# Attention and a gated feed-forward block on one core: first batch's q loaded whole behind k, its kv products and norms in another order

## The chip, the cores and the metric

The kernel runs on one core of a Trainium2 chip. The metric is the device time of one execution in microseconds (us). The core has a matrix engine (TensorE, PE in the profile, whose weight loads are listed apart as PEld), VectorE (DVE), ScalarE (ACT), GpSimd (POOL) and SyncE (SP), which here only issues transfers. TensorE writes to PSUM, a small memory from which DVE and ACT read; everything else lies in SBUF. Transfers from and to main memory run on 16 DMA engines, which the queues of SP, ACT and POOL share.

## The reference

```
kv  = einsum('bhsd,bhse->bhde', k, v)          # 8 batches, 8 heads, 576 rows, 64 wide
out = einsum('bhsd,bhde->bhse', q, kv)
rms = sqrt(mean(out*out, -1) + 1e-6)
x   = (out / rms * g_norm) as (4608, 512)
xn  = x / sqrt(mean(x*x, -1) + 1e-6) * moe_rms_g
h   = silu(xn @ w_gate) * (xn @ w_val)         # 512 -> 1536
y   = h @ w_out                                # 1536 -> 512
```

Inputs and output are float32; the kernel's matrix products take bfloat16.

## The kernel before, in words

Each batch's 576 rows are taken as four chunks of 128 rows (512 rows, "main") and a rest of 64. The 8 heads go in four pairs j = 0 to 3; P0 is pairs 0 and 1 (heads H0, 0 to 3), P1 is pairs 2 and 3 (H1, 4 to 7). The feed-forward block works on groups of 512 rows, one group for each batch and a ninth for the rests. Its weights come in four blocks of three 128-column slices (`wg`, `wv`, each loaded and cast to bfloat16 by transfers of the POOL queue), wo likewise.

In the steady part a list of slots, each a gate or value product or a part of the output product, is run in order on TensorE, and a planner (`Placer`) puts the pieces of the next batch's attention into slots by cost. The change does not touch that part. It touches the lead, lines 814 to 931, where the order is written out by hand (`manual_schedule`): an engine runs its instructions in the order in which the code issues them.

Batch 0's lead, in the order of the code: POOL issues the loads of v's rest (`vr`, "remv") and v's main part in two halves of heads, cast on the way (814, 815). SP loads k's heads H0, ACT k's H1 (816, 817), then SP q's chunks 0 and 1 of all heads (818), ACT the rest of k (`krst`) and the gains (`grow`). The second half of q's columns (chunks 2 and 3) follows on SP and ACT (826 to 828) with a dependency: not before v's rest has landed. POOL then makes the identities, issues the eight weight loads (832) and clears some tiles (833 to 836).

TensorE turns over an idle tile (`spin`, 844 and inside `kv_pairs`) until v is there. Then: kv of P0 in one PSUM tile (`kva`, 850), q's chunks 0 and 1 turned for both halves (`qa`, `qb`, 851), the gains turned (`gT`), kv of P1 in one tile (`kvb`, 854). DVE masks kv to its diagonal blocks on the way out (`kv_pairs_out`, kvs). `oT_mm` makes the transposed attention output, which ACT squares (`sqT_`); `stat_pairs` sums the squares by head into a PSUM tile `st`, over a guard product that holds the epsilon; `lead_chain` turns these sums into one factor `al` per row and head (reciprocal, product, sum, product on DVE, square root on ACT, reciprocal on DVE); `o_pairs` makes the output again in row order, `xna_pairs` scales it, `xT_mm` turns it, and `xT_out` writes x with the gain. All of this is for chunks 0 and 1 only. The gates of the first three slices on these 256 rows (`gates`, line 712) follow at once.

Chunks 2 and 3 come behind: `early` is a list of 22 half-width gate and value slots in the order gates of block 0, values of block 0, gates of block 1 and so on, and `behind(n)` issues a piece of their attention behind slot n: at 0 the late q is turned (`qT_mm(ALL, (2, 3))`) and copied, at 2 and 3 oT and its squares, at 5 the sums, at 5 to 9 the chain of scales (`steps`), at 7 and 8 o, at 11 and 12 xna, at 14 and 15 xT. POOL casts the late q (887, 888) and issues batch 1's loads (889 to 891) ahead of wo's.

PSUM pools: `mm1` three tiles, `o2` two, `att` three; a tile is taken again when its last reader is done.

Of the kernel before, what the change touches and what calls it, by code (L numbers as in the profile page):

```python
# [10 lines left out]
FP32 = mybir.dt.float32  # L11
# [3 lines left out]
OP = mybir.AluOpType  # L15
ACT = mybir.ActivationFunctionType
SYNC = mybir.DependencyInfo(mybir.DependencyClass.Sync, mybir.DependencyReason.DATA)
# [70 lines left out]
def kernel(  # L88
# [12 lines left out]
    nc = tc.nc  # L101
    B, H, S, D = q.shape
    d_model = H * D
    d_ff = moe_w_gate.shape[1]
    eps = 1e-6
    NC = 4
    MAIN = 128 * NC
    REM = S - MAIN
    NS = d_model // 128
# [8 lines left out]
    pool = lambda name, bufs, **kw: ctx.enter_context(tc.tile_pool(name=name, bufs=bufs, **kw))  # L118
# [13 lines left out]
    mm1_p = pool("mm1", 3, space=bass.MemoryType.PSUM)  # L132
    o2_p = pool("o2", 2, space=bass.MemoryType.PSUM)
    att_p = pool("att", 3, space=bass.MemoryType.PSUM)
# [8 lines left out]
    gall = consts.tile([128, NS + 1], FP32, name="gall")  # L143
    vc, kc = ([consts.tile([128, H, (NC + 1) * D], BF16, name=f"{t}c{n}") for n in range(2)] for t in "vk")
    sel = consts.tile([128, 2, 2], BF16, name="sel")
    qc = consts.tile([128, H, (NC + 1) * D], BF16, name="qc1")
    diag = consts.tile([128, 2 * D], BF16, name="diag")
    ones = consts.tile([1, 128], FP32, name="ones")
    epsr = consts.tile([1, (NC + 1) * H], FP32, name="epsr")
    gain = consts.tile([128, NS], FP32, name="gain")  # L150
# [5 lines left out]
    kvs = [consts.tile([128, NS, 2, D], BF16, name=f"kvs{n}") for n in range(3)]  # L156
# [24 lines left out]
    def load_main(b, t, heads=(0, H), cs=(0, NC), queue=nc.sync):  # L181
        if (b, t) not in staged:
            staged[b, t] = stage.tile([128, H, NC * D], FP32, name="stg")
        h0, h1 = heads
        view = src[t][b, :, 0:MAIN, :].rearrange("h (p c) d -> p h (c d)", c=NC)
        return queue.dma_start(
            out=staged[b, t][:, h0:h1, cs[0] * D : cs[1] * D], in_=view[:, h0:h1, cs[0] * D : cs[1] * D]
        )
# [17 lines left out]
    def cast_main(b, t, eng, heads=(0, H), cs=(0, NC)):  # L206
        if (b, t) not in mains:
            mains[b, t] = qkv.tile([128, NC, H, D], BF16, name=f"main_{'qkv'[t]}")
        h0, h1 = heads
        copy = eng.copy if eng is nc.scalar else eng.tensor_copy  # L210
        return copy(  # L211
            out=mains[b, t][:, cs[0] : cs[1], h0:h1, :],
            in_=staged[b, t].rearrange("p h (c d) -> p c h d", c=NC)[:, cs[0] : cs[1], h0:h1, :],
        )
# [23 lines left out]
    def spin(ps, n):  # L238
        for _ in range(n):
            nc.tensor.matmul(ps, lhsT=idle[:, :128], rhs=idle[:, : ps.shape[-1]], start=True, stop=True, skip_group_check=True)  # L240
# [4 lines left out]
    class Att:  # L245
# [34 lines left out]
                            start=c == 0, stop=c == NC, skip_group_check=True,  # L280
                        )

        def kv_pairs(self, js, wait=0):
            ps = mm1_p.tile([128, 4, 2 * D], FP32, name="mm1")
            spin(flat(ps), wait)
            ps = ps[:, : len(js)]
            for i, j in enumerate(js):
                for c in range(NC + 2):
                    h = slice(2 * j, 2 * j + 2)
                    if c < NC:  # L290
                        k_, v_ = self.pair(1, c, j), self.pair(2, c, j)
                    else:
                        k_, v_ = krT[:, c - NC, h, :], vr[:, h, c - NC, :]
                    nc.tensor.matmul(
                        ps[:, i, :], lhsT=k_, rhs=v_,
                        start=i == 0 and c == 0, stop=i == len(js) - 1 and c == NC + 1, skip_group_check=True,
                    )
            return ps
# [121 lines left out]
            src = ps.rearrange("p j (c t) -> p j c t", t=128)  # L420
            nc.scalar.activation(out=to, in_=src, func=ACT.Square)

        def stat_pairs(self, js, c0, c1, pool, name, guard=False):
            first = self.st is None
            if first:
                self.st = pool.tile([128, 2, NC + 1, H], FP32, name=name)
                if guard:
                    nc.tensor.matmul(
                        self.st[:, 0, c0:c1, :], lhsT=ones, rhs=epsr[:, : (c1 - c0) * H], start=True, stop=True,
                        skip_group_check=True,  # L430
                    )
                    first = False
            for c in range(c0, c1):
                for j in js:
                    nc.tensor.matmul(
                        self.st[:, :, c, 2 * j : 2 * j + 2], lhsT=self.sqT[:, j, c], rhs=sel,
                        start=first, stop=True, skip_group_check=True,
                    )
                    first = False
# [370 lines left out]
    V, G, A = nc.vector, nc.gpsimd, nc.scalar  # L810
# [2 lines left out]
    ALL = range(NS)  # L813
    v_loads = [G.dma_start(out=vr[: REM // 2].rearrange("p h c d -> p h (c d)"), in_=two(2))]
    v_loads += [load_cast(0, 2, hsx) for hsx in (H0, H1)]
    load_main(0, 1, H0)
    load_main(0, 1, H1, queue=A)
    load_main(0, 0, cs=(0, 2))
    krst = stage.tile([128, H, NC * D], FP32, name="stg")[: REM // 2, :, : 2 * D]
    A.dma_start(out=krst, in_=two(1))  # L820
    A.preload_act_table(ACT.Sqrt)
# [1 line left out]
    for half in range(2):  # L823
        A.dma_start(out=grow[NS : NS + 1, half * D : (half + 1) * D], in_=g_norm.rearrange("(o d) -> o d", o=1))

    for hsx, queue in ((H0, nc.sync), (H1, A)):
        rest = load_main(0, 0, hsx, cs=(2, 4), queue=queue)
        tc.add_manual_dep(rest.ins, v_loads[0].ins.name, SYNC, reason="k and v have the queues first")

    make_identity(nc, ident)  # L830
    make_identity(nc, identf)
    w_loads = [load_w(n) for n in range(len(FB))]
    G.memset(kvs[0], 0.0)
    G.memset(kvs[1], 0.0)
    for tile_ in (kc[0], kc[1], vc[0], vc[1], qc):
        G.memset(tile_[REM:, :, NC * D :], 0.0)

    def fold(w, s, eng):
        if eng == "ACT":
# [1 line left out]
        else:  # L841
            V.tensor_scalar(out=w[:, s], in0=w[:, s], scalar1=gain[:, s : s + 1], scalar2=None, op0=OP.mult)

    spin(mm1_p.tile([128, MAIN], FP32, name="mm1"), 18)
    a = Att(0)
    cast_main(0, 1, V, H0)
    cast_main(0, 1, A, H1)
    V.tensor_copy(out=krT[: REM // 2], in_=krst.rearrange("p h (c d) -> p c h d", c=2))
    cast_main(0, 0, V, cs=(0, 2))
    kva = a.kv_pairs(P0, 4)  # L850
    qa, qb = (a.qT_mm(js, (0, 1)) for js in (P0, P1))
    gT = o2_p.tile([128, NS + 1], FP32, name="o2")
    nc.tensor.matmul(gT, lhsT=grow, rhs=identf, is_transpose=True, start=True, stop=True, skip_group_check=True)
    kvb = a.kv_pairs(P1)
    for i, j in enumerate(P0):
        a.kv_pairs_out(kva, i, j)
    a.qT_out(qa, P0, 0, A)
    a.qT_out(qb, P1, 0, V)
    V.tensor_copy(out=gall, in_=gT)
    gcol = gall[:, NS : NS + 1]  # L860
    for half in range(2):
        rows = slice(half * D, (half + 1) * D)
        V.tensor_tensor(out=sel[rows, 1, half : half + 1], in0=gcol[rows], in1=gcol[rows], op=OP.mult)
    ta = a.oT_mm(P0, 0, 2, o2_p)
    a.sqT_(ta, P0, 0, 2)
    for i, j in enumerate(P1):
        a.kv_pairs_out(kvb, i, j)
    V.tensor_scalar(
        out=gain, in0=gall[:, 0:NS], scalar1=gcol, scalar2=float(d_model) ** 0.5, op0=OP.mult, op1=OP.mult
    )  # L870
    for i, j in enumerate(P1):
        a.sqT_(a.oT_mm((j,), 0, 2, (o2_p, mm1_p)[i], 4 * (1 - i)), (j,), 0, 2)
    a.stat_pairs(P0, 0, 2, mm1_p, "mm1", guard=True)
    a.stat_pairs(P1, 0, 2, mm1_p, "mm1")
    ox = a.o_pairs(P0, 0, 2, att_p, "att")
    oy = a.o_pairs(P1, 0, 2, att_p, "att")
    a.lead_chain(0, 2)
    spin(mm1_p.tile([128, MAIN], FP32, name="mm1"), 5)
    for o, js in ((ox, P0), (oy, P1)):
        for i, j in enumerate(js):  # L880
            a.xna_pairs(o[:, :, 2 * i : 2 * i + 2], (j,), 0, 2)

    for j, pool_, eng in zip(ALL, (o2_p, o2_p, None, None), (A, V, A, V)):
        a.xT_mm((j,), (0, 1), pool_)
        a.xT_out(j, (0, 1), eng)

    for hsx in (H0, H1):
        cast_main(0, 0, G, hsx, cs=(2, 4))
    for t in (0, 2, 1):
        load_cast(1, t, (0, H))  # L890
        load_cast(1, t)
# [10 lines left out]
        early += [slots_a(0, j, 0, half)[0] for j in js if n] + [slots_a(0, j, 0, half)[1] for j in js]  # L902
    held = {}

    steps = {5: (0, 4), 7: (4, 6), 8: (6, 8), 9: (8, 12)}

    def behind(n):
        if n == 0:
            ps = a.qT_mm(ALL, (2, 3))
            a.qT_out(ps[:, 0:2], P0, 2, V)  # L910
            a.qT_out(ps[:, 2:4], P1, 2, V)
        elif n in (2, 3):
            js = (P0, P1)[n - 2]
            a.sqT_(a.oT_mm(js, 2, 4, o2_p), js, 2, 4)
        elif n == 5:
            a.st = None
            a.stat_pairs(P0, 2, 4, att_p, "att")
            a.stat_pairs(P1, 2, 4, att_p, "att")
        if n in steps:
            for f in a.chain(2, NC)[slice(*steps[n])]:  # L920
                f()
        if n in (7, 8):
            held[n - 7] = a.o_pairs((P0, P1)[n - 7], 2, 4, att_p, "att")
        if n in (11, 12):
            i = (11, 12).index(n)
            a.xna_pairs(held[i], (P0, P1)[i], 2, 4)
        elif n in (14, 15):
            i = (14, 15).index(n)
            a.xT_mm((P0, P1)[i], (2, 3), None if i else o2_p)
            for j in (P0, P1)[i]:  # L930
                a.xT_out(j, (2, 3), A)
# [83 lines left out]
```

## Time and profile before

| | |
|---|---|
| median of 3 runs | 322.69 us (321.81 to 322.73) |
| the profiled execution | 321.78 us |
| its span in the profile | 320.0 us |
| TensorE busy | 313.0 us (98%) |
| VectorE, ScalarE, GpSimd busy | 176.3, 142.3, 90.8 us |
| granted TensorE clock | 1.00 |
| DMA moved | 40.57 MB, mean 127 GB/s |

The span is what the profile covers; 1.78 us of the execution lie around it. A busy share is an average over the whole span: the lead is some 5% of it and has limits of its own, so what the change is worth is read from the first 30 us. In a timeline line the columns are start, length, engine, source line, operation, out<-in with tile names, shape and count, and in brackets the engine's idle time before it and what ended that. Lines such as L684 are helpers' lines: the product of gates and values stands there whoever calls it.

### The profile page before, as it was taken

To read this page: it belongs to the slowest core of one execution; us is meant where nothing else is said; L and a number is where in the kernel's file an instruction comes from. 1 tells how busy PE (TensorE), PEld (TensorE's weight loads), DVE (VectorE), ACT (ScalarE), POOL (GpSimd) and SP (SyncE) were. 2 spreads that over 40 slices of the span, in tenths; PEclk is the share of its full clock that TensorE was granted. 3 is DMA by queue.
4 is the path that set the end of the run, shared out by engine and by line. 5 is a ranking of instruction groups with operands and counts; after the bars stand their busy time and mean duration, and the time that the engine had idled before them with its cause. 6 is when DMAs were issued, how large, how long until landed. Compare 5 with 4: busy or idle time off the path is not lost.

```text
span 320.0 us, 5586 instructions
## 1 busy us (share of the span) xinstructions
PE 313.0 (98%) x2142; PEld 159.3 (50%) x2142; DVE 176.3 (55%) x395; ACT 142.3 (44%) x263; POOL 90.8 (28%) x113
## 2 busy tenths in 40 slices
PE   8799999999999999999999999999999999999996
PEld 3588865444454445444444444444444444444443
DVE  4665538589949661967186817691778043203410
ACT  1465456486668323832292228322742233223321
POOL 8753530069008500860077006800510000000000
PEclk9999999999999999999999999999999999999999
DMA  8999999999783985497549955995000600040002
GB/s 215 221 203 197 195 230 209 200 214 110 141 206 93 155 165 144 113 146 147 137 149 123 155 146 154 105 139 151 34 3 0 172 35 0 6 106 21 0 33 100
DMA packets 78934, 40.57 MB, mean 127 GB/s; under 512 B 42552, under 2 KB 74428, under 8 KB 78908
## 3 DMA queue, kind: packets, MB, share of 16 engines
q0 software_dynamic: 31200, 14.22, 34.9%
q1 hardware_dynamic: 46224, 25.01, 32.0%
q10 hardware_dynamic: 1484, 0.99, 1.0%
q8 instruction: 17, 0.28, 0.4%
q14 instruction: 9, 0.07, 0.1%
HBM read 37.78 MB, written 9.44 MB: 148 GB/s over the span
## 4 chain that ended last, share of the span: by engine, by line
PE 91%; DMA 8%; issue 0%; DVE 0%; ACT 0%; POOLq 0%
PE mm L684 57%; PE o L719 27%; DMA wv<-in_moe_w_val_dram 5%; DMA remv<-in_v_dram 2%; PE att L278 2%; PE mm L719 2%; PE att L349 1%; PE o L362 1%; PE att L362 0%; PE mm L746 0%; PE o L746 0%; PE att L324 0%; PE att L558 0%; PE att L410 0%; PE att L445 0%
## 5 line engine op out<-in xcount | busy, mean ns | idle before, releaser
L702 DVE TENSOR_TENSOR h<-silu,mm 128x512 bf16<-128x512 bf16 (+1 forms) x120 | 75.4, 630 | 84.6 <-PE mm L684 75.2
L693 ACT ACTIVATE silu<-mm 128x512 bf16<-128x512 f32 (+1 forms) x120 | 66.5, 557 | 83.2 <-PE mm L684 74.3
L684 PE MATMUL mm<-x,wv 128*128 128x512 bf16 (+1 forms) x432 | 99.9, 356 | 0.2 <-DMA wv<-in_moe_w_val_dram 0.2
L684 PE MATMUL mm<-x,wg 128*128 128x512 bf16 (+1 forms) x420 | 97.9, 358 | 0.0
L719 PE MATMUL o<-wo,h 128*128 128x512 bf16 x396 | 90.0, 379 | 0.0
L452 POOL TENSOR_TENSOR sq<-sq,g 128x512 bf16<-128x512 bf16 x31 | 35.4, 1151 | 126.5 <-ACT sq L397 126.5
L684 PEld LDWEIGHTS <-wv 128*128 128x128 bf16 x480 | 46.2, 98 | 45.4 <-DMA wv<-in_moe_w_val_dram 0.5
L684 PEld LDWEIGHTS <-wg 128*128 128x128 bf16 x468 | 45.1, 98 | 44.9 <-DMA wg<-in_moe_w_gate_dram 0.2
L719 PEld LDWEIGHTS <-h 128*128 128x128 bf16 x420 | 40.2, 98 | 45.8
L735 ACT COPY osb<-o 128x512 f32<-128x512 f32 x33 | 19.2, 586 | 69.2 <-PE o L719 67.2
L460 DVE TENSOR_REDUCE st<-sq 128x8 f32<-128x512 bf16 x62 | 39.7, 677 | 0.2
L307 DVE CAST kvs<-att 64x256 bf16<-64x256 f32 x14 | 5.9, 422 | 28.7 <-PE att L278 28.1
L527 DVE TENSOR_TENSOR xna<-outa,al 128x512 bf16<-128x512 bf16 x24 | 15.1, 683 | 0.0
L684 PE MATMUL mm<-xr,wv 128*128 128x512 bf16 x48 | 12.3, 379 | 0.0
L684 PE MATMUL mm<-xr,wg 128*128 128x512 bf16 x48 | 12.3, 379 | 0.0
L397 ACT ACTIVATE sq<-att 128x512 bf16<-128x512 f32 x19 | 11.7, 618 | 0.0
L401 ACT CAST outa<-att 128x512 bf16<-128x512 f32 x19 | 11.5, 604 | 0.0
L211 POOL CAST main_q<-stg 128x1024 bf16<-128x1024 f32 (+1 forms) x12 | 11.3, 971 | 0.6 <-DMA stg<-in_q_dram 0.6
L240 PE MATMUL mm<-idle 128*128 128x512 bf16 x27 | 8.7, 492 | 1.2 <-DVE idle L138 1.2
L840 ACT ACTIVATE wv<-wv,gain 128x384 bf16<-128x384 bf16 x16 | 9.0, 608 | 0.4 <-PE mm L684 0.4
L197 POOL DMA_DIRECT2D vc<-in_v_dram x9 | 7.7, 860 | 0.3 <-DMA wg<-in_moe_w_gate_dram 0.3
L719 PE MATMUL mm<-wo,h 128*128 128x512 bf16 x24 | 7.8, 379 | 0.0
(138 smaller groups left out, 187.6 us busy)
## 6 DMA issues: line engine op xcount, KB each, us to landing
out_dram<-osb SPq DMA_DIRECT2D x31, 256.0 KB, 2.5
stg<-in_q_dram SPq DMA_DIRECT2D x6, 1024.0 KB, 7.9
vc<-in_v_dram POOLq DMA_DIRECT2D x7, 512.0 KB, 8.1
kc<-in_k_dram POOLq DMA_DIRECT2D x7, 512.0 KB, 6.4
wg<-in_moe_w_gate_dram POOLq DMA_DIRECT2D x4, 384.0 KB, 14.9
wv<-in_moe_w_val_dram POOLq DMA_DIRECT2D x4, 384.0 KB, 16.2
wo<-in_moe_w_out_dram POOLq DMA_DIRECT2D x4, 384.0 KB, 13.0
out_dram<-osb SPq DMA_DIRECT2D x9, 128.0 KB, 2.3
```

Source lines behind the costliest of these rows:

```text
L211: return copy(out=mains[b, t][:, cs[0] : cs[1], h0:h1, :], in_=staged[b, t].rearrange("p h (c d) -> p c h d", c=NC)[:, cs[0] : cs[1], h0:h ...
L397: nc.scalar.activation(out=self.sq[c][:, 0], in_=self.o_of(c), func=ACT.Square)
L401: nc.scalar.copy(out=self.outa[c], in_=self.o_of(c))
L452: eng.tensor_tensor(out=self.sq[c][:, 1], in0=self.sq[c][:, 0], in1=g2, op=OP.mult)
L460: nc.vector.reduce_sum(out=self.part(self.st[:, which], c), in_=of, axis=AX.X)
L527: return eng.tensor_tensor(out=self.part(self.xna, c), in0=self.outa[c].rearrange("p (c h) d -> p c h d", c=2), in1=self.part(self.al, c). ...
L684: nc.tensor.matmul(ps[:, : c1 - c0], lhsT=w[n][:, s, jj * 128 : (jj + 1) * 128], rhs=x_of(g, s, c0, c1), start=s == 0, stop=s == NS - 1)
L693: nc.scalar.activation(out=sis[g, j][:, c0:c1], in_=ps, func=ACT.Silu)
L702: nc.vector.tensor_tensor(out=hs[g, j][:, c0:c1], in0=sis[g, j][:, c0:c1], in1=v_ps, op=OP.mult)
L719: nc.tensor.matmul(ps, lhsT=hs[g, j][:, t * 128 : (t + 1) * 128], rhs=wo[j // OB][:, j % OB, :], start=j == 0, stop=j == NF - 1)
L735: (eng.copy if eng is nc.scalar else eng.tensor_copy)(out=o, in_=ps)
L840: A.mul(out=w[:, s], in_=w[:, s], mul=gain[:, s : s + 1])
```

## The change

q of batch 0 is loaded whole, in two halves of heads on SP, right behind k, which is loaded in four quarters of two heads that alternate between SP and ACT; the dependency on v's rest is gone. The casts of q's chunks 0 and 1 are split by heads between DVE and ACT; chunks 2 and 3 are cast by POOL right after the weight issues, the gain is computed on POOL instead of DVE, and the clearing of tiles moves behind the lead. TensorE's order becomes: kv of P0, q of P0 turned, gT, the guard, q of P1 turned, oT of P0, kv of pair 2 and of pair 3 in a tile each (one from `mm1`, one from `att`), oT of each, the sums, o, then the late q turned, then spins (3 instead of 5; 24 instead of 18 at the start, and the 4 ahead of pair 2's oT are gone). xT is made by pairs of heads in `o2` tiles. The copies of the late q stand behind xT's. The pieces behind the early slots move up by one to two slots.

```diff
-        def kv_pairs(self, js, wait=0):
-            ps = mm1_p.tile([128, 4, 2 * D], FP32, name="mm1")
+        def kv_pairs(self, js, wait=0, pool=None):
+            ps = (pool or mm1_p).tile([128, 4, 2 * D], FP32, name="att" if pool else "mm1")
...
-        def stat_pairs(self, js, c0, c1, pool, name, guard=False):
+        def guard(self, c0, c1):
+            self.st = mm1_p.tile([128, 2, NC + 1, H], FP32, name="mm1")
+            nc.tensor.matmul(
+                self.st[:, 0, c0:c1, :], lhsT=ones, rhs=epsr[:, : (c1 - c0) * H], start=True, stop=True,
+                skip_group_check=True,
+            )
+
+        def stat_pairs(self, js, c0, c1):
             first = self.st is None
             if first:
-                self.st = pool.tile([128, 2, NC + 1, H], FP32, name=name)
-                if guard:
-                    nc.tensor.matmul(
-                        self.st[:, 0, c0:c1, :], lhsT=ones, rhs=epsr[:, : (c1 - c0) * H], start=True, stop=True,
-                        skip_group_check=True,
-                    )
-                    first = False
+                self.st = att_p.tile([128, 2, NC + 1, H], FP32, name="att")
...
-    load_main(0, 1, H0)
-    load_main(0, 1, H1, queue=A)
-    load_main(0, 0, cs=(0, 2))
+    for n in range(NS):
+        load_main(0, 1, (2 * n, 2 * n + 2), queue=A if n % 2 else nc.sync)
+    for hsx in (H0, H1):
+        load_main(0, 0, hsx)
...
-    for hsx, queue in ((H0, nc.sync), (H1, A)):
-        rest = load_main(0, 0, hsx, cs=(2, 4), queue=queue)
-        tc.add_manual_dep(rest.ins, v_loads[0].ins.name, SYNC, reason="k and v have the queues first")
-
     make_identity(nc, ident)
     make_identity(nc, identf)
     w_loads = [load_w(n) for n in range(len(FB))]
-    G.memset(kvs[0], 0.0)
-    G.memset(kvs[1], 0.0)
-    for tile_ in (kc[0], kc[1], vc[0], vc[1], qc):
-        G.memset(tile_[REM:, :, NC * D :], 0.0)
...
-    spin(mm1_p.tile([128, MAIN], FP32, name="mm1"), 18)
+    spin(mm1_p.tile([128, MAIN], FP32, name="mm1"), 24)
...
-    cast_main(0, 0, V, cs=(0, 2))
+    cast_main(0, 0, V, H0, cs=(0, 2))
+    cast_main(0, 0, A, H1, cs=(0, 2))
     kva = a.kv_pairs(P0, 4)
-    qa, qb = (a.qT_mm(js, (0, 1)) for js in (P0, P1))
+    qa = a.qT_mm(P0, (0, 1))
     gT = o2_p.tile([128, NS + 1], FP32, name="o2")
     nc.tensor.matmul(gT, lhsT=grow, rhs=identf, is_transpose=True, start=True, stop=True, skip_group_check=True)
-    kvb = a.kv_pairs(P1)
+    a.guard(0, 2)
+    qb = a.qT_mm(P1, (0, 1))
     for i, j in enumerate(P0):
         a.kv_pairs_out(kva, i, j)
-    a.qT_out(qa, P0, 0, A)
-    a.qT_out(qb, P1, 0, V)
+    a.qT_out(qa, P0, 0, V)
     V.tensor_copy(out=gall, in_=gT)
     gcol = gall[:, NS : NS + 1]
+    G.tensor_scalar(
+        out=gain, in0=gall[:, 0:NS], scalar1=gcol, scalar2=float(d_model) ** 0.5, op0=OP.mult, op1=OP.mult
+    )
+    for hsx in (H0, H1):
+        cast_main(0, 0, G, hsx, cs=(2, 4))
+    a.qT_out(qb, P1, 0, V)
+    a.sqT_(a.oT_mm(P0, 0, 2, o2_p), P0, 0, 2)
+    made = [a.kv_pairs((j,), pool=pool_) for j, pool_ in zip(P1, (None, att_p))]
+    for ps, j in zip(made, P1):
+        a.kv_pairs_out(ps, 0, j)
...
-    ta = a.oT_mm(P0, 0, 2, o2_p)
-    a.sqT_(ta, P0, 0, 2)
-    for i, j in enumerate(P1):
-        a.kv_pairs_out(kvb, i, j)
-    V.tensor_scalar(
-        out=gain, in0=gall[:, 0:NS], scalar1=gcol, scalar2=float(d_model) ** 0.5, op0=OP.mult, op1=OP.mult
-    )
-    for i, j in enumerate(P1):
-        a.sqT_(a.oT_mm((j,), 0, 2, (o2_p, mm1_p)[i], 4 * (1 - i)), (j,), 0, 2)
-    a.stat_pairs(P0, 0, 2, mm1_p, "mm1", guard=True)
-    a.stat_pairs(P1, 0, 2, mm1_p, "mm1")
+    for j, pool_ in zip(P1, (o2_p, mm1_p)):
+        a.sqT_(a.oT_mm((j,), 0, 2, pool_), (j,), 0, 2)
+    a.stat_pairs(P0, 0, 2)
+    a.stat_pairs(P1, 0, 2)
     ox = a.o_pairs(P0, 0, 2, att_p, "att")
     oy = a.o_pairs(P1, 0, 2, att_p, "att")
     a.lead_chain(0, 2)
-    spin(mm1_p.tile([128, MAIN], FP32, name="mm1"), 5)
+    late = a.qT_mm(ALL, (2, 3))
+    spin(mm1_p.tile([128, MAIN], FP32, name="mm1"), 3)
...
-    for j, pool_, eng in zip(ALL, (o2_p, o2_p, None, None), (A, V, A, V)):
-        a.xT_mm((j,), (0, 1), pool_)
-        a.xT_out(j, (0, 1), eng)
-
-    for hsx in (H0, H1):
-        cast_main(0, 0, G, hsx, cs=(2, 4))
+    for js in (P0, P1):
+        a.xT_mm(js, (0, 1), o2_p)
+        for j, eng in zip(js, (A, V)):
+            a.xT_out(j, (0, 1), eng)
+    for n, js in enumerate((P0, P1)):
+        a.qT_out(late[:, 2 * n : 2 * n + 2], js, 2, V)
+
+    G.memset(kvs[0], 0.0)
+    G.memset(kvs[1], 0.0)
+    for tile_ in (kc[0], kc[1], vc[0], vc[1], qc):
+        G.memset(tile_[REM:, :, NC * D :], 0.0)
...
-    steps = {5: (0, 4), 7: (4, 6), 8: (6, 8), 9: (8, 12)}
+    steps = {4: (0, 4), 5: (4, 7), 6: (7, 9), 7: (9, 11), 8: (11, 12)}
...
-        if n == 0:
-            ps = a.qT_mm(ALL, (2, 3))
-            a.qT_out(ps[:, 0:2], P0, 2, V)
-            a.qT_out(ps[:, 2:4], P1, 2, V)
-        elif n in (2, 3):
-            js = (P0, P1)[n - 2]
+        if n in (0, 1):
+            js = (P0, P1)[n]
             a.sqT_(a.oT_mm(js, 2, 4, o2_p), js, 2, 4)
-        elif n == 5:
+        elif n == 4:
...
-        if n in (11, 12):
-            i = (11, 12).index(n)
+        if n in (9, 10):
+            i = (9, 10).index(n)
...
-        elif n in (14, 15):
-            i = (14, 15).index(n)
+        elif n in (12, 13):
+            i = (12, 13).index(n)
```

## The prediction

> **What bounds the kernel now.** I read the page's chain of waits first. It is 91% TensorE and 8% DMA, and VectorE, ScalarE and GpSimd set nothing in it. So TensorE alone is busy to the end once the DMA part is over. Where that is, the chain in order of time says (start, length, what):
>
> ```profile
> 1.31 7.19 DMA remv<-in_v_dram
> 8.51 0.28 issue
> 8.79 17.06 DMA wv<-in_moe_w_val_dram
> 25.89 1.05 PE mm L684 x8
> 26.94 0.22 PE o L558 x4
> ...
> 27.83 8.89 PE mm L684 x80
> ```
>
> The reader is to see that up to 25.89 us the end hangs on the weights' landing, not on the first batch's attention: the third block of w_val lands at 25.85, and from there TensorE runs without a gap. The list of waits gives TensorE only small ones there, 0.23 us for wv at 25.89; the timeline has 0.16 us for wg just ahead of 27.81. So the lead is almost exactly as long as the weights: gain in one is lost at the other unless both come earlier. I take 27.81 us, the first gate of the fourth block, as the point to shift; behind it the work is the same in both kernels.
>
> Then the timeline, for the lead's own steps:
>
> ```profile
> 10.32 0.38 PE L294 MATMUL mm<-vc,main_k 128*128 128x128 bf16 x4 [1.66 <-DMA vc<-in_v_dram]
> 12.36 0.38 PE L410 MATMUL o<-qTs,kvs 128*128 128x256 bf16 x2
> 14.31 0.26 DVE L478 RECIPROCAL r<-mm 128x16 f32<-128x16 f32 x1 [0.72 <-PE mm L435]
> 17.42 1.47 PE L712 MATMUL mm<-x,wg 128*128 128x256 bf16 x12
> 18.73 0.61 PE L313 MATMUL att<-ident,main_q 128*128 128x128 bf16 x8
> ```
>
> TensorE stands 1.66 us for v's first half, which lands at 10.3; the reciprocal of the statistics starts 4.0 us later, the first gate 3.11 us after that, and the late q (chunks 2 and 3) is turned behind the first gates, on the path.
>
> Last, the DMA view, asked for one microsecond at a time (queue: packets, MB, share). q0 is GpSimd's, with v and the weights; q1 is SyncE's, q10 ScalarE's. Here are 4 to 5, 10 to 11, 14 to 15 and 17 to 18 us:
>
> ```profile
> q10 hardware_dynamic: 211, 0.22, 60.7%
> q1 hardware_dynamic: 166, 0.16, 45.4%
> ...
> q0 software_dynamic: 377, 0.20, 144.5%
> ...
> q0 software_dynamic: 137, 0.10, 66.4%
> q1 hardware_dynamic: 134, 0.07, 33.4%
> q10 hardware_dynamic: 135, 0.07, 22.8%
> ...
> q0 software_dynamic: 261, 0.20, 128.9%
> ```
>
> The 16 engines have 16 us of time in each. k in 1 KB packets: 16/377 = 42.4 ns a packet. v in 512 B packets written: 16/377 = 42.4. Weights (768 B written) alone: 16/261 = 61 ns. Between 14 and 15 the three queues move equal numbers of packets; with 137 at 61 ns, the 269 packets of q, 512 B each, cost 28.4 ns. That a queue gets its turn by packets, not bytes, decides what follows.
>
> **q whole, behind k.** Before, q's row of 1 KB is read as two 512 B packets (2 x 28.4 = 56.8 ns); after, as one (42.4 at k's price). For 1024 rows that is 14.4 x 1024 / 16 = 0.92 us of DMA time saved ahead of the weights, so wv's third block at about 24.9 and wg's fourth at about 26.8 instead of 27.75. Bounds: nothing if price goes by bytes, 0.92 if by this count; I take the count, the rows being direct. [...]
>
> The price: q's second half (0.5 MB) had been held by a dependency until remv landed (issue at 8.53); now it stands ahead of v. By the per-microsecond counts GpSimd's queue begins at about 5.9 us and has sent 174, 212, 230 and 356 packets by 7, 8, 9, 10 us. remv is 256 and half of v is 512 packets, so the first half's last packet (768th) went at 9.4 and landed 0.9 later; the second's (1280th) at 10.8. At 6.0 us the old q had 351 small packets through; in large ones about 195, leaving 829. In turns of one each: remv, krst's 255 and 256 of q take (256 x 25 + 255 x 28.4 + 256 x 42.4)/16 = 1.53 us (25 ns for remv's small ones from the window 6 to 7), then v's half with 512 of q 2.71: to 10.24, **0.84 later**; the second half at 11.76, 0.96 later. Were all of q to pass first, 10.4 (+1.0); were v to get two packets to q's one, +0, but then q's own second half lands near 12.3 and its turn (qb) stands ahead of oT in TensorE's queue, so oT starts no earlier. I take +0.85: v at 11.15 and 12.5.
>
> **k in quarters.** Two more issues, 0.46 to 0.49 each on SP and ACT; k's first half lands over both queues. It waits for v in any case, whose landing is 4 us behind. ACT loses the issue that blocked it to 8.53, so its cast of k (9.04 before) comes near 6.5: also hidden. At best quarters let ACT's queue, whose first packets appear at 2.9 us against SP's 1.9, start sooner; bounds 0 to 0.45 us (0.9 us at half the rate), taken as 0.
>
> **The lead after**, from v at 11.15, with durations of before: kv of P0 to the first kvs product as before 0.89 (12.04), two products 0.49 (12.53). qT_out of qa moves from ACT to DVE behind them: 0.42 (12.97); its cover, ACT in parallel, is gone. oT of P0 at 13.0, its square on ACT 13.44 to 13.99. Only now kv of pair 2 and 3, six matmuls each (0.31): 13.2 to 13.82; each has a tile, so the products leave at 13.75 and 14.05 (0.25 each). oT of each 0.05 behind; squares 14.35 to 14.73, 14.73 to 15.1. The last statistics and the reciprocal 0.32 behind: 15.42, that is 4.27 after v instead of 4.0. The guard (0.39), gT and qb (0.25; its q half lands near 11.2, ACT's cast about 0.55, half of a 1.04 row) run on TensorE while it waits for DVE. From the reciprocal 3.11 as before: **first gate at 18.5 instead of 17.42**. xT by pairs in one tile may hold the first copy for the second xna (+0.17; that copy started at 16.74 when ACT's table load ended, so some is covered); lower bound 0, which I take.
>
> **Late q ahead.** Eight transposes cost TensorE 0.45 on the path (18.73 to 19.18, the next value matmul). After, they and three spins (0.64) lie in the 1.5 us from reciprocal to first xna. GpSimd must have cast the late q by then: its last weight issue waits for v's second half (12.5) and takes 0.74, gain at most 0.62 (DVE's row for the same operation), casts 1.17 in all: 15.0, before the turn at about 15.9. Its seven memsets (3.6) move behind, so batch 1's loads issue near 18.7 instead of 17.70; they queue behind the weights to 29.7 anyway, qc then landed 32.6 and is wanted at 36.65. DVE's two copies of the late q (0.76) precede the first h, which came 2.6 us after the first gate; DVE is free for 1.4 of them. The finer chain steps and earlier slots are the same instructions.
>
> **The sum.** First gate to 27.81 was 10.39. Minus 0.45 for the turn, minus the two waits, 0.39: 9.55. 18.5 + 9.55 = 28.05, and the weights (26.8) are there: **+0.24 us**. The profiled run took 321.78 (span 320.0 and 1.78 around it), 0.91 below the median 322.69; added to the median, **322.9**. A change under 0.3% (0.97 us) can't be told from none here.
>
> **Rivals.** (1) *Lead not delayed*: both queues start together (the 0.45 above) and v gets two packets to q's one, with q's half in by 11. v lands at 9.8, TensorE's spins (28 now, six more at 0.213: to 9.94) end as it comes, first gate 9.95 + 7.38 = 17.35, the point at 26.9, weights near 26.4: -0.9, **321.8**. For it: from 2 to 3 us only 177 GB/s flow, nearly all on SP's queue, against 338 to 375 once both run. Against: equal turns from 14 to 15.
> (2) *Slower: v kept back by q*, at GpSimd's queue. It sent nothing until k was nearly through (9 packets before 6.0). If hardware queues go first and a 1 KB packet costs 56.8 beside others, q's 829 take 2.94 us, krst and v 2.2: 11.15, landed 12.05, first gate 19.43, point 28.98: +1.17, **323.9**. It decides from a first gate later than 18.26 (27.81 - 9.55). Against: 174 software packets to 221 and 190 from 6 to 7.
> (3) *Half clock.* The spins ran 13 times at 427 ns before 213. Lead spins fall from 9 to 3; if the clock drops and 4 us of gates run at half speed, 2 us are lost: **324.9**. Against: granted clock 1.00 throughout, 1.66 us idle before 10.32 without harm. [...]
> (4) *Weights no earlier*: q's packets cost by their bytes, so wg's fourth block lands at 27.75 again. Then a first gate anywhere before 18.26 gains nothing, the point stays at 27.8 and the change does not do what it says: **322.7**. For it: the 0.16 us wait ahead of 27.81, which any earlier lead lengthens. Against: 42.4 against 56.8 ns for the same 1 KB.
>
> **Chances.** Forecast 0.40 (its own range 322.2 to 323.6), (1) 0.26, (2) 0.18, (3) 0.06, (4) 0.10. Faster by over 0.3%: 0.20 of (1)'s 0.26. Slower: 0.17 of (2), all of (3), 0.05 of the forecast's upper edge: 0.28. Within: 0.52. The range runs from 321.4, past (1), to 324.0, past (2); (3) is left out.
>
> **What would show it.** TensorE's wait for vc ending near 11.2; fewer than 10 packets of q0 before 6; the reciprocal 4.3 behind; first gate at 18.5; eight transposes ahead of it; no wait for wv or wg up to 28.05. Wrong if v lands by 10.3, if a wait for weights stays, or if gates run at 427 ns for 512 columns.

## The result and the profile after

| | before | after |
|---|---|---|
| median, 6 runs each | 322.25 us (321.64 to 323.04) | 325.70 us (324.52 to 326.51) |
| ratio | 1 | 1.0103 (95%: 1.0077 to 1.0128) |
| the profiled execution, its span | 321.78, 320.0 us | 324.87, 323.1 us |
| granted TensorE clock, mean of a run | 1.00 (profiled) | 0.995 (profiled); the six: 0.995, 0.984, 0.984, 0.984, 0.989, 0.994 |

The change makes the kernel 1.0% slower, 3.45 us by the medians. The chain of waits after, in order of time, begins like this (start, length, what):

```profile
2.09 9.82 DMA vc<-in_v_dram
11.95 0.83 PE mm L294 x12
13.43 0.54 PE att L313 x4
13.97 0.43 PE o L410 x2
14.40 0.64 PE mm L294 x6
```

The weights are gone from it: the end now hangs on the landing of v's first half and on the lead behind it. The timeline after, with the lines that answer to those of before (the kv matmuls of the first pair, oT, kv of pair 2, the reciprocal, the turn of the late q, the first gates):

```profile
11.95 0.38 PE L294 MATMUL mm<-vc,main_k 128*128 128x128 bf16 x4 [2.00 <-DMA vc<-in_v_dram]
...
13.77 0.63 PE L410 MATMUL o<-qTs,kvs 128*128 128x256 bf16 x2
14.19 0.63 PE L294 MATMUL mm<-vc,main_k 128*128 128x128 bf16 x4
...
17.20 0.26 DVE L479 RECIPROCAL r<-mm 128x16 f32<-128x16 f32 x1 [0.96 <-PE mm L436]
...
17.47 0.61 PE L313 MATMUL att<-ident,main_q 128*128 128x128 bf16 x8
...
20.43 1.53 PE L713 MATMUL mm<-x,wg 128*128 128x256 bf16 x12
```

v's kv starts 1.63 us later than before (11.95 against 10.32). The reciprocal follows 5.25 us behind it instead of 3.99, and the first gate stands 3.01 us later. The gate of the fourth block comes at 30.41 instead of 27.81, 2.60 later, and the batch 1 kv product, for instance, at 44.07 instead of 41.48, 2.59 later, and so does the last full-width copy of output (316.82 against 314.23): what is lost in the lead is lost to the end. The two profiled spans differ by 0.5 us more, which lies behind that copy, among the last stores, and has no explanation here. Four kv matmuls of one shape take 0.38 us at 11.95 and 0.63 at 14.19. The view by windows says why (window, its length, then busy time and instructions of PE, PEld, DVE, ACT and POOL, then the granted clock, the DMA share and GB/s):

```profile
11.70:13.40 1.70, 1.45 (x20) 1.30 (x20) 0.58 (x3) 0.62 (x1) 0.82 (x2) 0.95 1.37 202
13.40:15.10 1.70, 1.70 (x16) 1.57 (x16) 0.76 (x4) 0.60 (x1) 1.56 (x4) 0.50 1.31 202
15.10:16.80 1.70, 1.30 (x13) 0.73 (x10) 0.78 (x4) 0.69 (x2) 1.64 (x4) 0.55 1.31 202
```

For 3.4 us in the middle of the lead TensorE runs at half clock. In the window from 13.4 to 15.1 before, the clock was 1.00. A mean of 0.995 is what one such stretch makes (3.4 x 0.5 of 323 us); 0.989 and 0.984 are two and three of them (the trace of e9_gate, at 0.984, has three), and the runs with the lower clocks are the longer ones (325.29 at 0.989; 326.10 to 326.51 at 0.984; 324.52 and 324.87 at 0.994 and 0.995).

The DMA view from 8 to 9 us after (queue: packets, MB, share):

```profile
q0 software_dynamic: 165, 0.08, 60.8%
q1 hardware_dynamic: 169, 0.16, 59.5%
q10 hardware_dynamic: 29, 0.01, 4.6%
```

Before, v's queue sent 230 packets in this microsecond beside 194 small ones of q; now 165 beside 169 large ones. The counts are nearly equal, and each of q's packets is larger: 0.16 MB in 169 against 0.10 in 194.

### The profile page after: what moved, and what is told of

The parts are those of the page before. It is cut to its first block, busy times and chain, and to the rows that moved or that the text cites. A ratio compares the mean times of both kernels' runs of the same rounds, so it can differ in the third digit from the quotient of the medians.

```text
span 323.1 us, 5569 instructions
## 1 busy us (share of the span) xinstructions
PE 313.3 (97%) x2120; PEld 159.9 (50%) x2142; DVE 176.0 (54%) x395; ACT 142.6 (44%) x263; POOL 91.5 (28%) x114
## 3 DMA queue, kind: packets, MB, share of 16 engines
HBM read 37.78 MB, written 9.44 MB: 146 GB/s over the span
## 4 chain that ended last, share of the span: by engine, by line
PE 94%; DMA 3%; issue 1%; DVE 1%; ACT 0%; POOL 0%; DVEq 0%; POOLq 0%
PE mm L685 58%; PE o L720 26%; DMA vc<-in_v_dram 3%; PE att L278 2%; PE mm L720 2%; PE att L349 1%; PE o L362 1%; PE o L559 0%; PE mm L713 0%; PE mm L294 0%; PE att L362 0%; PE mm L747 0%; PE o L747 0%; PE att L324 0%; PE att L559 0%
## 5 line engine op out<-in xcount | busy, mean ns | idle before, releaser
L720 PE MATMUL o<-wo,h 128*128 128x512 bf16 x382 | 88.1, 379 | 1.2 <-issue 0.8
L528 DVE TENSOR_TENSOR xna<-outa,al 128x512 bf16<-128x512 bf16 x24 | 15.1, 682 | 0.0
L240 PE MATMUL mm<-idle 128*128 128x512 bf16 x30 | 9.4, 482 | 1.2 <-DVE idle L138 1.2
```

The costliest lines, as they stand in the source:

```text
L528: return eng.tensor_tensor(out=self.part(self.xna, c), in0=self.outa[c].rearrange("p (c h) d -> p c h d", c=2), in1=self.part(self.al, c). ...
L720: nc.tensor.matmul(ps, lhsT=hs[g, j][:, t * 128 : (t + 1) * 128], rhs=wo[j // OB][:, j % OB, :], start=j == 0, stop=j == NF - 1)
```

## The experiments

Ratios are against the kernel before, run on the same chip beside them.

| run | median us | before, same chip | ratio (95%) |
|---|---|---|---|
| e1_spins | 323.88 | 321.88 | 1.0054 (1.0037 to 1.0071) |
| e2_order | 321.97 | 321.88 | 1.0001 (0.9987 to 1.0016) |
| e3_loads | 323.60 | 321.88 | 1.0049 (1.0032 to 1.0065) |
| e4_halves | 323.24 | 321.88 | 1.0034 (1.0022 to 1.0046) |
| e5_sel | 323.22 | 322.04 | 1.0036 (1.0026 to 1.0046) |
| e6_slots | 323.22 | 322.04 | 1.0034 (1.0024 to 1.0043) |
| e7_spins25 | 321.83 | 322.04 | 0.9987 (0.9975 to 0.9998) |
| e8_spins12 | 324.58 | 322.04 | 1.0064 (1.0041 to 1.0086) |
| e9_gate | 329.47 | 321.91 | 1.0226 (1.0205 to 1.0248) |
| e10_quarters | 322.31 | 321.91 | 1.0003 (0.9991 to 1.0016) |
| e11_late1 | 322.01 (one run) | 321.91 | |

**More spins in the changed kernel.**

```diff
-    spin(mm1_p.tile([128, MAIN], FP32, name="mm1"), 24)
+    spin(mm1_p.tile([128, MAIN], FP32, name="mm1"), 33)
```

> The changed kernel with 33 spins instead of 24 ahead of the first kv product, nothing else: the idle 2.0 us of TensorE until v are filled (9 spins at 0.213 us end at about 11.9, where v lands at 11.95). Theory clock (a good part of the 1.0% is the half clock that follows the idle stretch): granted clock 1.00 in every run, the reciprocal about 4.3 to 4.5 us after the first kv product instead of 5.25, median 324.3 or less against 325.7 and the runs closer together than their 2 us. Theory DMA alone (v's lateness and the order are all of it): clock or not, median stays within 0.5 of 325.7.

The clock is 0.997 to 1.00 in all six runs, their spread falls from 2.0 to 1.1 us, and the ratio falls from 1.0103 to 1.0054. About half of the loss was the clock. The reciprocal still stands 4.83 us behind v (11.82 to 16.65), more than expected; two rows show what is left:

```profile
13.70 0.40 PE L313 MATMUL att<-ident,main_q 128*128 128x128 bf16 x4 [0.44 <-ACT main_q L211]
...
16.27 0.34 PE L436 MATMUL mm<-sel,sqT 128*128 128x4 bf16 x8 [0.61 <-DVE sel L868]
```

q's second half lands late enough for its turn to wait for the cast, with oT behind it in TensorE's queue; and the sums wait for `sel`.

**The new order alone.** The kernel before with TensorE's new order; loads, first spins, late q and early slots as before:

```diff
-    kvb = a.kv_pairs(P1)
+    a.guard(0, 2)
+    qb = a.qT_mm(P1, (0, 1))
...
+    a.sqT_(a.oT_mm(P0, 0, 2, o2_p), P0, 0, 2)
+    made = [a.kv_pairs((j,), pool=pool_) for j, pool_ in zip(P1, (None, att_p))]
```

> The kernel before with TensorE's new order alone (kv of pairs 2 and 3 in a tile each behind oT of P0, guard early, gain on GpSimd, xT by pairs; the loads, the 18 spins, the late q behind the first gates as before). Theory order harmless: v lands at 10.3 as before, reciprocal 4.0 after it, time within 0.3 us of before. Theory order costs (4.27 instead of 4.0 in the prediction): reciprocal 0.3 later, first gate near 17.7, +0.3 us. Theory clock: with 9 spins fewer in the lead's middle than before it may also fall to half clock although v is on time: then clock under 1.00 and +1 us or more.

No difference. With v at 10.09 the reciprocal starts 4.20 us behind it, near the predicted 4.27 against 3.99, at 14.29; the first gate follows it by 3.24 instead of 3.11, at 17.53 (before 17.42), and the third wv is waited for (0.32 us). So the order costs about 0.3 us in the lead, which the waits for weights take up. The clock dropped in 4 of its 12 runs, and in 8 of the 20 runs of before beside them.

**The new loads alone.** The kernel before with quarters of k, q whole and casts by heads, and 33 spins:

```diff
-    load_main(0, 1, H0)
-    load_main(0, 1, H1, queue=A)
-    load_main(0, 0, cs=(0, 2))
+    for n in range(NS):
+        load_main(0, 1, (2 * n, 2 * n + 2), queue=A if n % 2 else nc.sync)
+    for hsx in (H0, H1):
+        load_main(0, 0, hsx)
```

> The kernel before with the new loads alone (k in quarters, q whole behind it without the dependency, q's first casts split by heads) and 33 spins, so that TensorE is not idle before v. Theory loads: v lands near 11.9 (1.6 later than before) and takes the first gate with it, to 19.0 to 19.5; the weights land about 1 us earlier and are not waited for; +1.2 to +1.8 us. Theory order or clock: time within 0.5 us of before, since the order is the old one and the clock is kept busy.

v's kv starts at 11.37, 1.05 later; the first gate at 18.81, 1.39 later; +1.7 us by the medians. The loads are the other half of the loss, and they make it with the old order too.

**k in halves again, the rest of the change kept, 33 spins.**

```diff
-    for n in range(NS):
-        load_main(0, 1, (2 * n, 2 * n + 2), queue=A if n % 2 else nc.sync)
+    load_main(0, 1, H0)
+    load_main(0, 1, H1, queue=A)
```

> As the run with 33 spins, but k in two halves (SP, ACT) instead of quarters, q whole behind it on SP. If quarters help or harm v (they start ACT's queue 0.3 us earlier and let GpSimd's first packets in at 5 us and then out again), v's landing moves by over 0.3 us against that run; if they do nothing, landing and time agree within 0.3 us.

0.64 us less than with quarters by the medians, though the intervals of the two ratios overlap. In the traces v's kv is only 0.15 earlier, but q's second half lands 1.4 us earlier (its cast starts at 11.58 instead of 13.03), so its turn no longer waits, and the first gate moves from 19.88 to 19.11.

**k in quarters alone**, in the kernel before with 25 spins (same edit the other way):

> The kernel before with 25 spins and k in quarters, nothing else. Theory quarters harm: they let v's rest in at 5 us between k's packets and starve v at 6 to 7 us (9 to 39 packets there against 103 with halves), so v lands 0.2 us or more later than 10.3 and the time is 0.2 to 0.6 above 321.83. Theory harmless: v at 10.3, time within 0.2 us of the run with 25 spins.

```profile
10.96 0.38 PE L294 MATMUL mm<-vc,main_k 128*128 128x128 bf16 x4 [0.41 <-DMA vc<-in_v_dram]
...
18.37 1.47 PE L712 MATMUL mm<-x,wg 128*128 128x256 bf16 x12
```

The run with 25 spins and k in halves has there

```profile
10.33 0.38 PE L294 MATMUL mm<-vc,main_k 128*128 128x128 bf16 x4 [0.89 <-DMA vc<-in_v_dram]
...
17.43 1.47 PE L712 MATMUL mm<-x,wg 128*128 128x256 bf16 x12
```

v is 0.63 later than with halves and the first gate 0.94 later. The time is 0.48 above that run's median, taken on another chip, and as much above the ten runs of before on the same chip that lost no clock (321.83). All 12 runs with quarters stand at 0.998 or more, which hides this in the ratio of 1.0003: 7 of the 17 runs of before lost a stretch. Most of the 0.94 us does not reach the end: the fourth block's gate comes at 28.25, only 0.15 behind that run's, which waited for weights.

It is not that v's packets go later. remv's 253 packets go early, at 5 to 6 us between k's; from 6 to 7 the queue sends 12; but by 9.5 us it has sent 808 packets, against 763 in the run with 25 spins. What is longer is the way from there to the landing. The trace keeps, for each of these loads, 16 increments of its semaphore, and TensorE starts 0.04 us behind the last (10.28 and 10.32 before, 11.91 and 11.95 after). For v's first half they come from 9.35 to 10.92 us here, from 9.63 to 10.29 there. The eighth is no later (9.68 against 9.94); the last few are. In the 13 traces of this case the 16 lie 0.35 to 0.76 us apart in the nine kernels with k in halves and 0.96 to 1.57 in the four with quarters (0.76 in the kernel before, 9.52 to 10.28; 1.43 in the changed one, 10.48 to 11.91). So with quarters the last increments come later behind the first, and TensorE waits for the last. Why is not shown.

**Half of q held back.** e4_halves with one thing undone:

```diff
-    for hsx in (H0, H1):
-        load_main(0, 0, hsx)
+    load_main(0, 0, H0)
...
+    rest = load_main(0, 0, H1)
+    tc.add_manual_dep(rest.ins, v_loads[0].ins.name, SYNC, reason="k and v have the queues first")
```

> The run with k in halves and 33 spins, with one thing undone: q's second half of heads (SP) again waits until v's rest has landed. Theory q ahead of v: with half of q out of the way v lands before 10.8 instead of 11.7 (the spins then end at 11.9 and hide it in TensorE's start; the landing is read from GpSimd's issue that waits for it, 12.2 in the changed kernel and 10.56 before), and the price moves: q's second half lands near 13, its cast and turn (qb) stand ahead of oT, so the first gate is no earlier than 19.1 and the time no better than 323.2. Theory the DMA engines are simply slower in this kernel: v lands at 11.7 as well.

GpSimd's issue that waits for v's first half went out at 9.88 without waiting for it, so v had landed by then, 2 us ahead of e4_halves (where that issue goes at 11.87; 12.20 in the changed kernel). That q ahead of v delays v is shown. And the other half of the expectation holds more strongly than written:

```profile
17.45 0.60 PE L313 MATMUL att<-ident,main_q 128*128 128x128 bf16 x4 [5.47 <-ACT main_q L211]
```

q's second half lands at 16.7. Its packets appear from 12 us on, beside those of GpSimd's queue (56 and 227 from 12 to 13), and everything behind `qb` waits 5.5 us for it. Its turn stands 4.4 us later than in e4_halves (13.04). Against e4_halves the loss is 6.2 us by the medians, and the clock is the rest of it: it is at half from 14.20 to 24.43, three stretches, with 0.984 in all four runs, and from that turn to the first gate takes 7.8 us instead of 6.1. q and v take turns on the DMA engines (169 and 165 packets from 8 to 9 us in the changed kernel); whichever goes first, `oT` needs both, and k.

**The spins of the kernel before**, 25 and 12 instead of 18:

```diff
-    spin(mm1_p.tile([128, MAIN], FP32, name="mm1"), 18)
+    spin(mm1_p.tile([128, MAIN], FP32, name="mm1"), 25)
```

> The kernel before with 25 spins instead of 18 at the start: they end at 10.15 us, just ahead of v at 10.3, and the 1.66 us of idle are filled. Of the 20 runs of before beside the first four experiments, seven or so stand at 322.6 to 323.0 us (those listed with their clock at 0.995) and the rest at 321.7 to 322.1 (0.998 to 1.00). Theory clock by idleness: all runs at clock 0.998 or more and at 321.6 to 322.1 us, the upper group gone, median about 321.8. Theory chance: the upper group stays.

> The kernel before with 12 spins: they end at about 7.4, so TensorE idles 2.9 us until v. Theory clock by idleness: clock 0.984 to 0.995 in most runs and the time 0.9 to 2 us above before, with loads, order and late q as before. Theory lateness alone (the changed kernel is slow only for v): time as before, since nothing else waits for the spins.

With 25, all 11 runs have a clock of 0.999 or 1.00 and 321.76 to 322.30 us; of the 28 runs of before beside them 8 stand at 0.995 and 322.50 to 323.11. This is the one version below the kernel before, by 0.13%, and what it gains is that group. It did not fill the gap: in its trace TensorE still waits 0.89 us for v. With 12, every one of 6 runs is at 0.989 to 0.995, and the time is 2.5 us up with nothing changed but idle time. By the spans it is 1.5 us; in this version alone more time than elsewhere lies around the span (1.8 to 2.9 us, 1.7 to 1.9 in the others), which has no explanation here. In its trace TensorE waits 3.74 us for v, until 10.24, and runs at half clock from 11.46 to 14.88:

```profile
11.70:13.40 1.70, 1.70 (x16) 1.57 (x16) 0.92 (x6) 0.22 (x1) 1.67 (x3) 0.50 1.26 222
```

**sel ahead of the late cast.** e4_halves, with one line moved:

```diff
     gcol = gall[:, NS : NS + 1]
+    for half in range(2):
+        rows = slice(half * D, (half + 1) * D)
+        V.tensor_tensor(out=sel[rows, 1, half : half + 1], in0=gcol[rows], in1=gcol[rows], op=OP.mult)
```

> The run with k in halves and 33 spins, with DVE's two small products that fill sel moved ahead of the copy of qb, where GpSimd's cast of the late q has not begun. In that run they took 0.69 us behind kvs (0.32 in the run with the old loads, 0.98 in the run with quarters) and the first sum waited 0.32 us for them. Theory GpSimd in the way of DVE (the early cast of the late q slows DVE's products that the sums wait for): the two take 0.32, the wait for sel goes, reciprocal and first gate about 0.3 earlier, -0.3 us. Theory none of it: squares end as late as sel, nothing moves.

The two products take 0.33 us again instead of 0.69, and the wait for them is gone, but the reciprocal stays (15.93 against 15.87): the squares of pair 3 end no earlier. A miss; the slow `sel` is real and hidden.

**The old slots for chunks 2 and 3**, on top of that:

```diff
-        if n in (0, 1):
-            js = (P0, P1)[n]
+        if n in (2, 3):
+            js = (P0, P1)[n - 2]
...
-        elif n in (12, 13):
-            i = (12, 13).index(n)
+        elif n in (14, 15):
+            i = (14, 15).index(n)
```

> As the run with sel ahead, with the pieces of chunks 2 and 3 behind the early slots where they were before (oT behind 2 and 3, sums behind 5, xT behind 14 and 15), the late q still turned ahead of the first gate. Theory slots: the saving of 0.45 us for the late q did not show from first gate to the fourth block's gate (9.97 us against 10.0 before without its waits for weights) because xT, two slots earlier, waits 0.3 us for xna on TensorE; then first gate to that point takes 9.6 and the time falls by 0.3 to 0.4 us. Theory weights: their landing takes its place and nothing moves.

A miss as well: from the first gate to the fourth block's takes 9.91 us (19.13 to 29.04) instead of 9.99, and the time is the same. But a new wait shows up right behind the first gates:

```profile
20.91 1.03 PE L685 MATMUL mm<-x,wv 128*128 128x256 bf16 x8 [0.25 <-ACT silu L694]
```

**The late q one slot later**, in the kernel before with 25 spins:

```diff
-        if n == 0:
+        if n == 1:
             ps = a.qT_mm(ALL, (2, 3))
```

> The kernel before with 25 spins and the late q turned behind early slot 1 instead of 0. Theory cover (the late q cost nothing where it was, since right behind the first gates TensorE waits for the first silu to give a PSUM tile back): a wait for silu of 0.2 to 0.3 us appears ahead of the first values, and the gates of block 1 start 3.7 to 3.8 us after the first gate instead of 3.51. Theory path (it cost 0.45 there): no such wait, still 3.5.

```profile
17.76 1.15 PE L712 MATMUL mm<-x,wg 128*128 128x256 bf16 x9
19.16 0.60 PE L684 MATMUL mm<-x,wv 128*128 128x256 bf16 x4 [0.25 <-ACT silu L693]
19.59 0.61 PE L313 MATMUL att<-ident,main_q 128*128 128x128 bf16 x8
```

In the run with 25 spins and the late q in its old place:

```profile
18.74 0.61 PE L313 MATMUL att<-ident,main_q 128*128 128x128 bf16 x8
19.19 1.04 PE L684 MATMUL mm<-x,wv 128*128 128x256 bf16 x8
```

The next matmul behind the first gates could start at 18.74, as the late q's did there. Without it the first value product starts at 19.16, when the first silu has given a PSUM tile back, and with it at 19.19. So in that place the turn cost 0.03 us, not 0.45. The gates of block 1 come 4.16 us after the first, later than the expected 3.7 to 3.8, since oT then also waits for the late q's copies.

## Why the prediction was wrong, step by step

The fourth block's gate was forecast at 28.05 and came at 30.41. In the sum's own terms: v's kv 0.80 later than forecast (11.95, not 11.15), from there to the reciprocal 0.98 more (5.25, not 4.27), from that to the first gate 0.12 more (3.23, not 3.11), from there to the point 0.43 more (9.98, not 9.55). Of the signs named, the eight transposes ahead of the gate and the missing waits for weights came.

**The sum's first term, v at +0.85, was half of what it is.** That queues take turns by packets held: 165 packets of v beside 169 of q. Two of its sizes did not. By an estimate from the counts the 1 KB packet costs more beside v's than alone: from 9 to 10 us after, 163 of v at 42.4 ns leave 54 ns for each of q's 167, where 42.4 was taken. With 54 the prediction's own working puts the 768th packet at 10.8 (6.0 + 1.72 + 3.08) instead of 10.24, and with k in halves (e4) it goes at 10.78. In the changed kernel it goes at 10.35 (704 by 10 us, 179 in the next microsecond), near the forecast 10.24, but that is luck: the queue had sent 267 packets before 6 us, where fewer than 10 were expected, because k came in quarters. The other size is the landing: 0.9 us behind that packet was taken over from before. It holds with halves (0.8 in e4); with quarters it is 1.56 (11.91), and 1.0 to 1.5 in e1, e3 and e10.

**k in quarters was taken at nothing, with bounds from 0 to 0.45 us of gain.** No bound lay on the side of a loss. Alone they delay v's landing by 0.63 us (e10), and in the changed kernel q's second half by 1.4 (e1 against e4).

**The clock was the step that failed worst.** The prediction gave half clock 0.06, on the ground that 1.66 us of idle did no harm before. Its own numbers had 1.2 us (spins to 9.94, at 213 ns each where the traces show 216; v at 11.15); v's lateness made them 2.0. And one profiled run at 1.00 was read as the rule: of the 65 runs of before beside the experiments, 23 had lost a stretch of clock (322.5 to 323.1 us). The median that the forecast started from, 322.69, lies among these, 0.91 above the profiled run. What was called harmless was a matter of luck at 1.66 us, and at 2.0 us it happened in all six runs. The price was right in kind: e1 takes 1.8 us off the median, where the prediction gave 2 us. By the runs, rival 3 came, set off by a v as late as rival 2 had it (11.9 against its 12.05), and the range, which left the clock out, ended 1.7 us too low. Rival 2's price per packet was near (56.8, against 54 by the counts); its mechanism, hardware queues first, was not: from 9 to 10 us q's queue sent 167 packets and v's 163.

**The late q saved nothing.** Its 0.45 us were read as path because TensorE was busy there. They covered a wait for silu (e11). After, first gate to the fourth block's takes 9.98 us, predicted 9.55, before 10.0 without its waits for weights.

**The weights came earlier by half of the sum's term.** GpSimd's wo issue that waits for wg's fourth block goes at 27.58 after and 28.05 before: 0.47 instead of 0.92, and nobody waited for it. What the whole rows save in DMA time stays unused as long as the lead is the later of the two.

**The order was priced rightly up to the reciprocal** (4.27 behind v predicted, 4.20 in e2). The 0.17 that xT by pairs might cost was taken at its lower bound, 0; it is 0.13 (3.23 to 3.24 from reciprocal to first gate in after, e1, e2 and e4, 3.10 to 3.11 in before, e3, e7 and e10). The harmless moves on GpSimd were harmless, except that its early cast of the late q slows `sel` (0.98 us in e1, 0.69 in e4, 0.33 ahead of the cast in e5), which was not foreseen; putting it right moved nothing in e5.

In sum, by medians: the clock 1.8 us (after to e1), quarters 0.6 (e1 to e4), and the rest, q ahead of v above all, 1.4 (e4 to the runs of before beside it): 3.8. The 3.45 measured first stand against six runs of before of which three lie at 322.7 to 323.0, where runs with a lost stretch lie. The 54 ns of a 1 KB packet beside v's are an estimate from packet counts; that quarters spread the increments of v's landing (1.57 us in e10, 0.66 in e7) is measured. Why is left open in both.

## What to carry to other kernels

Where TensorE waits for a first load, fill most of the wait: a gap of 2 us cost a half-clock stretch in every run and one of 1.66 us in a third of them (23 of 65), while in versions whose traces show 0.4 to 0.9 us left (e3, e7, e10) none of 29 runs lost one. One profiled run doesn't show that; the clocks of all runs do. Here loads shared the DMA engines by turns, and larger packets beside v's left it fewer (230 packets of v from 8 to 9 us beside q's small ones, 165 beside its large ones), so a load that the first product needs should not stand beside one that could wait. Look at when a load lands, not only at when its packets go: splitting k moved the one and not the other. Before you count an instruction on a busy engine as path, ask what the engine would wait for without it.

## What the runs showed of the hardware

The clock: stretches of 3.41 us at 0.50 (0.995, 0.989, 0.984 for one, two, three in 323 us). In the three traces that have them, the drops stand at no one distance from the start of the gap: 3.27 us behind it in the changed kernel (9.95 to 13.22), 4.96 with 12 spins (6.50 to 11.46), 2.22 in e9_gate (11.98 to 14.20). From where the clock first came up, when the spins go from 427 to 216 ns, they are two, two and three times 3.41 us away: from 6.39 to 13.22 in the changed kernel, from 4.64 to 11.46 with 12 spins, from 3.96 to 14.20 in e9_gate. In these three, TensorE was busy for 1.42, 1.22 and 1.19 us of the 3.41 ahead of the drop. Counted in steps of 3.41 us from the same point, the least busy stretch in the lead that no drop followed had 1.87 (with 12 spins), and in the traced run of before the gap is split between two, with 2.27 and 2.89. The clock came back after a stretch with 3.18 us busy (after) or 3.41 (12 spins, e9_gate), and not after one with 2.88 (e9_gate). Where it first comes up changes from run to run (3.96 us in e9_gate, 4.64 with 12 spins, 6.39 in before and after), and so does the end of the first spins: the same 29 end at 9.44 us in e7 and at 10.54 in e10. An estimate from these numbers: 3.41 us that hold the whole 1.66 us gap of before have 1.75 us of work left, between 1.42 and 1.87, which would fit a loss in some runs of before and not in others. No run of before that lost a stretch was traced, and more on when the clock drops than these three drops is not shown.

VectorE beside GpSimd: in e1 the two 64x1 products of `sel` took 0.98 us and ended when GpSimd's cast of the late q did (16.21 and 16.20), in e4 0.69 us, ending with the cast at 15.39; in e5, ahead of the cast, they took 0.33, and in the changed kernel, beside a GpSimd memset, 0.32. Why they take longer beside the cast is not shown. First e1, then after:

```profile
15.23 0.98 DVE L868 TENSOR_TENSOR sel<-gall 64x1 bf16<-64x1 f32 x2
...
15.04 1.16 POOL L211 CAST main_q<-stg 128x512 bf16<-128x512 f32 x2
...
15.58 0.52 POOL L889 MEMSET kvs<- 128x512 bf16 x1
...
15.93 0.32 DVE L868 TENSOR_TENSOR sel<-gall 64x1 bf16<-64x1 f32 x2
```
